# Moving the down-projection's weight combinations in four pieces, loading raw w_down one section ahead, and reordering the last groups of an attention-plus-GeGLU kernel

## The chip, the cores and the metric

The kernel runs on one core of a Trainium2 chip. The core has five engines that run side by side and meet at semaphores: TensorE (PE in the profile; its weight loads are PEld), VectorE (DVE), ScalarE (ACT), GpSimd (POOL) and SyncE (SP). In this kernel SP issues every DMA, one after the other, in the order of the program. The metric is the device time of one execution in microseconds (us), the median over several runs.

## The reference

With x of 2048 tokens by 576 features, all in float32:

```python
xn = layernorm(x)                                  # no scale, no bias
q, k, v = split(xn @ wqkv)                         # 32 heads of 18
s = softmax(q @ k.T * 18 ** -0.5) @ v  @ wo        # no mask
g = silu((gelu(xn @ w_gate) * (xn @ w_up)) @ w_down)   # hidden width 4608
out = x + s * g
```

## The kernel before

The float32 products are made of two reduced-precision parts each: a value is cut into a high part and a remainder, and three products (high with high, high with remainder, remainder with high) are summed in PSUM. Cutting is work of ACT, POOL and DVE.

**Prologue.** Layer norm, transposes, and the projections to q, k and v, whose results go to DRAM (`qk`, `vs`). The transposed, cut activations go to DRAM too (`xhs`).

**Sections.** The feed-forward part is cut into 144 sections: 4 token blocks of 512 tokens by 36 slices of 128 hidden columns. A section (`section`) multiplies one block with one slice of w_gate and w_up in 27 pairs of matmuls. Its number n gives the block b, the unit r (two slices, so 18 units for a block) and the half g of the unit: g = 0 is even n. Each section asks for the raw gate and up slices of section n + 2 (`load_gu`, 576 KB in two DMAs into two `raw` buffers) and has POOL (ACT in the lead) cut those of the next section, `split_gu`. Behind its pairs come the activation and `finish`, which sums and cuts the hidden values (`sums_a`, `cut_a`) into the tile A.

**Down products.** A unit's contribution to the output of the block is made by `down`: seven products instead of eight for a two by two split of the matrices, with combinations of quarters. They run one section after the unit's second one, so behind the even section of the next unit. The combinations of the w_down quarters are in the tile T: two precisions (index i) of seven combinations, 2016 KB. In block 0 the first five units (`PLAIN`) use the quarters as they are. The 18 units of `FORMED` (the other 13 units of block 0 and the first 5 of block 1) form T from the raw slice (`rawd`): `sums_b` on POOL makes the sums (`tsum`), `high_b` on ACT cuts the high parts, `low_b` on POOL the remainders, and `store_t` writes T to DRAM (`ts`). All other units read T back from there with `load_t`. Seven accumulators lie in M and are updated by DVE after each product; `combine` and `gates` bring them together at the end of a block and send them to DRAM (`ys`).

**Attention between the pairs.** From section 11 to section 138 the 27 pairs of a section have 8 score products (`score_pair`, their exponentials on ACT) and 8 products for the row maxima (`max_pair`, reduced by DVE) between them; the products with v (`values`) follow. All of them, the down products and the last projection take turns in three PSUM buffers (`ring`). Sections 0 to 10 are the lead, sections 139 to 143 the ends. Keys are loaded seven chunks ahead (`load_k`), and each such load waits for the scores of an older chunk, so SP walks through the program about one section at a time. The 32 units of attention results are normalised later: `load_scale` loads a unit and its reciprocal sums, `scale` multiplies on POOL, `store_scale` writes back (`on`).

**Block change.** In the last section of a block the activations of the next block are loaded (`load_xd`, six DMAs of 384 KB) and copied to the other half of the partitions by ACT and POOL (`copy_xd`).

**Ends.** Sixteen groups of 128 tokens are projected with wo (`project_o`, 28 matmuls each, after `split_o` has cut its input). `gate` takes tanh of the feed-forward result `yy`, `load_xy` loads x and `ys` of a group, and the sum goes to `out`. Twelve groups are spread behind the last sections, the block of the last four is special: its feed-forward result is still in M.

**What sets the order.** PE and SP run exactly in program order. The other engines' instructions are ordered ahead of time by a planner that simulates the program, apart from those marked `keep`, which stay in program order. A hook runs a piece of work in front of a given pair of the next section; on SP, where nothing waits for the pairs, a hook only sets a place in the queue.

## Time and profile before

| | |
|---|---|
| median of three runs | 2677.72 us (2675.94 to 2678.8) |
| profiled execution, its time | 2671.98 us |
| its span, first to last instruction | 2670.2 us |
| PE busy | 2573.9 us, 96% |
| DVE, POOL, ACT busy | 2146.0, 1585.5, 1476.0 us |
| mean granted PE clock | 0.988 |
| DMA | 442.85 MB, 166 GB/s |

Busy time of PE is the time in which at least one matmul is under way, so at 96% only about 96 us of the span are left in which it does nothing. A window row gives, for a stretch of time, its length, the busy time of each engine with the number of instructions, the granted clock, the mean busy share of the DMA engines and their rate. A timeline row gives start, duration, engine, line, operation and tiles, and in square brackets the idle time of the engine ahead of it and what ended it. A wait row gives who waited for whom, the total, how often, and the longest.

### The profile page before, as it was taken

The numbers are of one execution on the slowest core, as the hardware profiler recorded it, in microseconds if no ns is written. First come the engines' busy times: TensorE is split into PE (matmuls) and PEld (weight loads), VectorE is DVE, ScalarE is ACT, GpSimd is POOL, SyncE is SP. The second block draws the span as 40 slices with busy tenths as digits, with TensorE's granted clock in tenths as the row PEclk, the third lists the DMA queues.
The fourth block names the chain that finished last, engine by engine and source line by source line (L and its number), as shares of the span: only waits on it lengthen the run. The fifth ranks groups of instructions, "written<-read, shape, count | busy, mean of one in ns | idle before, by whom it ended". The sixth has DMA issues, their size and how long they took to land. (4 is left out here: it accounts for less than half of the span.)

```text
span 2670.2 us, 52622 instructions
## 1 busy us (share of the span) xinstructions
PE 2573.9 (96%) x20548; PEld 1850.8 (69%) x20548; DVE 2146.0 (80%) x2462; ACT 1476.0 (55%) x1783; POOL 1585.5 (59%) x1604
## 2 busy tenths in 40 slices
PE   9998999999999999999989999999999999999978
PEld 8886766666666666666656666666666666667667
DVE  5325788888887898999868989988987888997467
ACT  3223266666666655555556566666555656666522
POOL 2124478888788856566655655555566555555641
PEclk9999999999999999999989999999999999999989
DMA  8764355555566556665566555555565555554584
GB/s 263 260 222 128 92 150 161 156 161 156 156 178 177 164 174 166 166 165 165 165 150 176 166 157 156 156 156 156 156 171 159 160 148 158 157 158 139 143 248 143
DMA packets 378935, 442.85 MB, mean 166 GB/s; under 512 B 103484, under 2 KB 283196, under 8 KB 370112
## 3 DMA queue, kind: packets, MB, share of 16 engines
q1 hardware_dynamic: 378688, 439.49, 58.3%
q8 instruction: 163, 2.67, 0.4%
q14 instruction: 84, 0.69, 0.1%
HBM read 344.12 MB, written 95.26 MB: 165 GB/s over the span
## 5 line engine op out<-in xcount | busy, mean ns | idle before, releaser
L757 DVE TENSOR_REDUCE mx<-pm 128x2 f32<-128x1024 f32 x1024 | 1221.3, 1225 | 221.0 <-PE pm L756 201.8
L794 ACT ACTIVATE pT<-pe 128x1024 f32<-128x1024 f32 x1024 | 1047.4, 1027 | 611.0 <-PE pe L793 577.8
L421 PE MATMUL pu<-xd,wh 64*128 64x512 f32 x2538 | 931.7, 399 | 11.3 <-POOL xd L147 8.1
L421 PE MATMUL pg<-xd,wh 64*128 64x512 f32 x2538 | 931.3, 398 | 11.7 <-DMA xd<-xhs 6.0
L421 PEld LDWEIGHTS pg<-xd,wh 64*128 64x128 f32 x2538 | 471.2, 186 | 128.0 <-issue 60.3
L421 PEld LDWEIGHTS pu<-xd,wh 64*128 64x128 f32 x2538 | 470.9, 186 | 39.8 <-POOL xd L147 10.0
L421 PE MATMUL pg<-xd,wl 64*128 64x512 f32 x1269 | 498.4, 393 | 0.0
L421 PE MATMUL pu<-xd,wl 64*128 64x512 f32 x1269 | 497.8, 392 | 0.0
L106 POOL TENSOR_SCALAR wh<-raw 128x384 fp32r<-128x384 f32 x402 | 218.1, 547 | 448.2 <-DMA raw<-in_B_w_up_dram 234.3
L810 PE MATMUL acc<-pT,VS 128*32 128x512 f32 x4096 | 466.0, 595 | 0.0
L756 PE MATMUL pm<-KA,QT 64*128 64x512 f32 x2048 | 417.8, 396 | 16.3 <-ACT pT L794 15.4
L108 POOL TENSOR_TENSOR wl<-raw,wh 128x384 fp32r<-128x384 f32 x402 | 415.5, 1038 | 26.0
L793 PE MATMUL pe<-QT,KA 64*128 64x512 f32 x2048 | 418.3, 397 | 12.8 <-DVE mx L757 8.2
L533 PE MATMUL py<-T,ah 128*128 128x288 f32 x1876 | 384.7, 301 | 10.9 <-DVE M L537 8.5
L537 DVE TENSOR_TENSOR M<-py,M 128x576 f32<-128x576 f32 x448 | 338.9, 757 | 35.1 <-PE py L533 21.9
L533 PEld LDWEIGHTS py<-T,ah 128*128 128x128 f32 x1876 | 300.9, 190 | 66.6 <-issue 56.3
L450 POOL TENSOR_TENSOR al<-h,ah 128x512 fp32r<-128x512 f32 (+1 forms) x139 | 286.3, 2060 | 83.0 <-ACT ah L447 58.3
L810 PEld LDWEIGHTS acc<-pT,VS 128*32 128x32 f32 x4096 | 120.1, 109 | 276.7 <-issue 229.7
L793 PEld LDWEIGHTS pe<-QT,KA 64*128 64x128 f32 x2048 | 196.4, 185 | 130.1 <-DVE mx L757 29.3
L533 PE MATMUL py<-T,al 128*128 128x288 f32 x938 | 277.2, 296 | 2.4 <-POOL al L450 2.4
L421 PEld LDWEIGHTS pg<-xd,wl 64*128 64x128 f32 x1269 | 235.8, 186 | 32.3
L756 PEld LDWEIGHTS pm<-KA,QT 64*128 64x128 f32 x2048 | 202.5, 186 | 66.5 <-ACT pT L794 24.7
(155 smaller groups left out, 2984.0 us busy)
## 6 DMA issues: line engine op xcount, KB each, us to landing
T<-ts SPq DMA_DIRECT2D x49, 2016.0 KB
KA<-qk SPq DMA_DIRECT2D x768, 72.0 KB
raw<-in_B_w_gate_dram SPq DMA_DIRECT2D x144, 288.0 KB
raw<-in_B_w_up_dram SPq DMA_DIRECT2D x144, 288.0 KB
ts<-T SPq DMA_DIRECT2D x18, 2016.0 KB
VS<-vs SPq DMA_DIRECT2D x128, 152.0 KB
qk<-t SPq DMA_DIRECT2D x72, 256.0 KB
QT<-qk SPq DMA_DIRECT2D x192, 72.0 KB
```

What stands on the lines that cost most here:

```text
L106: first = nc.gpsimd.tensor_scalar(hi, raw, 1.0, 1.0, op0=ALU.mult, op1=ALU.mult)
L108: keep(nc.gpsimd.tensor_tensor(lo, raw, f(hi), op=ALU.subtract))
L421: nc.tensor.matmul(o, w[1 + wp][k][rr, c, :], xd[k][xp][rr, c, :], start=(i == 0), stop=(i == len(terms) - 1))
L450: keep(two.tensor_tensor(lo, raw, f(hi), op=ALU.subtract))
L533: nc.tensor.matmul(py[:, t, 0:DC], h[:, i, tt], T[:, w, k], start=n == 0, stop=n == 2)
L537: nc.vector.tensor_tensor(M[:, m], py[:, :, 0:DC], M[:, m], op=ALU.add)
L756: nc.tensor.matmul(pm[:, a], QS[u, r][rr, t * P:(t + 1) * P], KS[(u * NA + c) % KB][r][rr, :], start=True, stop=True)
L757: nc.vector.tensor_reduce(MX[u][:, 2 * r:2 * r + 2, t, c], pm, axis=AX.X, op=ALU.max)
L793: nc.tensor.matmul(pe[:, a], KS[(u * NA + c) % KB][r][rr, t * P:(t + 1) * P], QS[u, r][rr, :], start=True, stop=True)
L794: nc.scalar.activation(PT[u, kt][:, 2 * r:2 * r + 2, :], pe, AF.Exp, scale=SCALE)
L810: nc.tensor.matmul(ACC[u][32 * a:32 * a + 32, :], VS[(u * NA + c) % VB][:, v:v + 32], pt[:, a, :], start=first, stop=last, skip_group_chec ...
```

## The change

Eight things are changed, in the order of the program:

- `load_k(0)` and `load_q(0)`, 14 DMAs on SP, stand behind section 0 and its loads instead of ahead of them.
- Raw w_down of unit r + 1 is loaded in `finish` of the second section of unit r (`load_rawd`), not at the start of the next section behind its `load_gu`. `sums_b` is hooked to pair 12 instead of 22.
- T moves in four pieces (`PIECES`: for each precision the combinations 3 to 6 and then 0 to 2). The store is spread: the high parts at pairs 13 and 20 of the unit's second section, the remainders at pairs 2 and 9 of the section after it. The load has its first piece where the whole load stood and three at pairs 5, 13 and 21 of the next section. For the last unit of a block (blocks 1 and 2), all four pieces go one section later, to pairs 1, 6, 11 and 16 of the first section of the next block.
- The tiles of `load_scale` have two slots; it is called ahead of a section's maxima and down products, not near a block change; `scale` comes behind the down products of the next section instead of ahead of its maxima.
- The last reciprocal has a tile of its own (`t2`), and its store to DRAM is issued behind section 139 instead of ahead of the loads of the ends.
- Two groups of x and `ys` instead of one are loaded at the start of the ends; a group's load stands behind the projection of the group two earlier. `yy` has three buffers, and holds the gated product; `th` has one.
- The last unit's down products stand in front of all four groups of the last block instead of behind the first of them, then the four gates.
- The last block's groups are finished one at a time by DVE straight from PSUM, with one add and one store each.

```diff
+NEXT = [(0, r) for r in range(1, PLAIN)] + FORMED + [(0, NR)]
+PIECES = ((0, 3, 7), (0, 0, 3), (1, 3, 7), (1, 0, 3))
...
-    def load_t(r):
-        nc.sync.dma_start(f(FF["T"]).rearrange("p i m d -> p (i m d)"), ts[r])
+    def t_piece(r, k, store=False):
+        i, a, b = PIECES[k]
+        t, d = f(FF["T"])[:, i, a:b].rearrange("p m d -> p (m d)"), ts[r][:, (7 * i + a) * DC:(7 * i + b) * DC]
+        nc.sync.dma_start(*((d, t) if store else (t, d)))
...
+    def load_rawd(r):
+        FF["rawd"] = ffn.tile([P, G, D], F32, name="rawd")
+        nc.sync.dma_start(FF["rawd"], w_down[r * G * P:(r + 1) * G * P, :].rearrange("(g p) n -> p g n", p=P))
...
-        hooks, FF["hooks"] = FF["hooks"], {}
+        hooks, FF["hooks"], FF["next"] = FF["hooks"], FF["next"], {}
...
-        if g == 0 and (b == 0 or (b, r) in FORMED):
-            raw = FF["rawd"] = ffn.tile([P, G, D], F32, name="rawd")
-            nc.sync.dma_start(raw, w_down[r * G * P:(r + 1) * G * P, :].rearrange("(g p) n -> p g n", p=P))
-            if (b, r) in FORMED:
-                hook(22, lambda: sums_b(raw))
+        if n == 0:
+            load_rawd(0)
+        if g == 0 and (b, r) in FORMED:
+            raw = FF["rawd"]
+            hook(12, lambda: sums_b(raw))
...
+        if g == 1 and (b, r + 1) in NEXT:
+            load_rawd((r + 1) % NR)
...
+                for k, i in enumerate((13, 20)):
+                    hook(i, lambda k=k: t_piece(r, k, True))
...
-                store_t(r)
+                for k, i in enumerate((2, 9)):
+                    hook(i, lambda k=k: t_piece(r, 2 + k, True))
...
-                load_t(r)
+                late = (n + 2) % (NR * G) == 0 and n + 2 < NF
+                for k, i in enumerate((1, 6, 11, 16) if late else (None, 5, 13, 21)):
+                    if i is None:
+                        t_piece(r, k)
+                    else:
+                        hook(i, lambda k=k: t_piece(r, k), ("hooks", "next")[late])
...
+        if not SC:
+            SC.extend(ffn.tile([P, 2, TB], F32, name=m, tag=t) for m, t in (("on", "rawd"), ("od", "tsum")))
...
         def last_sums(u, rt):
-            rec = att.tile([P, QD, TB], F32, name="rec", tag="pT", bufs=4)[:, 0, :]
+            rec = ffn.tile([P, TB], F32, name="rec", tag="t2")
             tc.keep_in_program_order(nc.vector.reciprocal(rec, SUM[u]))
-            nc.sync.dma_start(rt, rec.rearrange("(a p) t -> a p t", p=32)[:, 0, :])
+            todo["rec"] = [lambda: nc.sync.dma_start(rt, rec.rearrange("(a p) t -> a p t", p=32)[:, 0, :])]
...
-        load_k(0)
-        load_q(0)
...
+            if n == 0:
+                load_k(0)
+                load_q(0)
...
+            if FF["n"] % G == 1 and (scaled + 1) * NA + 4 < n and SCALED <= n < NU * NA - 2 and 2 < FF["n"] % (NR * G) < NR * G - 2:
+                load_scale(scaled)
+                at(n + 1, 2, scale, scaled)
+                at(n + 2, 0, store_scale, scaled)
+                scaled += 1
...
-            if n >= SCALED and FF["n"] % G == 1 and (scaled + 1) * NA + 4 < n < NU * NA - 2:
-                load_scale(scaled)
-                at(n + 1, 0, scale, scaled)
...
-                nc.vector.scalar_tensor_tensor(th, th, 1.0, yy, op0=ALU.add, op1=ALU.mult)
+                nc.vector.scalar_tensor_tensor(yy, th, 1.0, yy, op0=ALU.add, op1=ALU.mult)
...
-                S2[j] = epi.tile([P, 2, DC], F32, name="s", tag=("yy", "th")[j % 2], bufs=2)
-                nc.scalar.activation(S2[j], po[:, :, 0:DC], AF.Copy, scale=0.25)
+                t = epi.tile([P, D], F32, name="last", tag="yy", bufs=3)
+                for c in range(2):
+                    m = QUARTERS[2 * (j // 2) + c][2]
+                    nc.vector.scalar_tensor_tensor(t[:, DC * c:DC * c + DC], FF["M"][:, m, j % 2], 0.25, po[:, c, 0:DC],
+                                                   op0=ALU.mult, op1=ALU.mult)
+            (nc.vector if (b, j) == groups[-1] else nc.gpsimd).tensor_tensor(xx, xx, t, op=ALU.add)
...
+        load_xy(*groups[0])
         load_wo()
+        load_xy(*groups[1])
...
+        def step():
+            nonlocal n
+            n += 1
+            ready()
+            project_o(*groups[n - 1])
+            if n + 1 < len(groups):
+                load_xy(*groups[n + 1])
+            if n > 1:
+                store()
...
+            if i == 0:
+                todo.pop("rec")[0]()
...
-        for k in range(TB // P):
-            if k == 1:
-                downs(then)
-            n += 1
-            ready()
-            project_o(*groups[n - 1])
+        downs({6: ((6, sub, 3),), 0: ((6, add, 0), (5, add, 0), (5, add, 2)), 4: ((6, sub, 4), (4, add, 2)),
+               1: ((5, sub, 1), (1, sub, 3))})
         M = FF["M"]
-        TG = [ffn.tile([P, 2, 2, DC], F32, name="tg", tag=tag) for tag in ("rawd", "tsum")]
-        for q, (i, c, m) in enumerate(QUARTERS):
-            t = TG[q // 2][:, q % 2]
+        for i, c, m in QUARTERS:
+            t = ffn.tile([P, 2, DC], F32, name="tg", tag=("h0", "h1")[c], bufs=2 - c)
             nc.scalar.activation(t, M[:, m], AF.Tanh, scale=0.25)
-            nc.vector.scalar_tensor_tensor(t, t, 1.0, M[:, m], op0=ALU.add, op1=ALU.mult)
-            for a in range(2):
-                j = 2 * i + a
-                nc.vector.tensor_tensor(t[:, a], t[:, a], S2[j][:, c], op=ALU.mult)
-                xx = XY[NB - 1, j][0][:, DC * c:DC * c + DC]
-                (nc.vector, nc.gpsimd)[a].tensor_tensor(xx, xx, t[:, a], op=ALU.add)
-                if c == 1:
-                    nc.sync.dma_start(out[S - TB + j * P:S - TB + (j + 1) * P, :], XY[NB - 1, j][0])
+            nc.vector.scalar_tensor_tensor(M[:, m], t, 1.0, M[:, m], op0=ALU.add, op1=ALU.mult)
+        for k in range(TB // P):
+            step()
+        store()
```

More of the change, by code (lines that the diff above doesn't have):

```diff
@@ L392 @@
     ps = ctx.enter_context(tc.tile_pool(name="ps", bufs=1, space=PSUM, reuse_waits="tile"))
-    FF = {"w": ahead, "xd": XD, "down": [], "gates": [], "n": 0, "hooks": {}, "raw": {},
+    FF = {"w": ahead, "xd": XD, "down": [], "gates": [], "n": 0, "hooks": {}, "next": {}, "raw": {},
           "M": ffn.tile([P, 7, 2, DC], F32, name="M"),
@@ L622, in finish, with hook @@
         FF.pop("last", lambda: None)()
-        def hook(i, what):
-            FF["hooks"].setdefault(i, []).append(what)
+        def hook(i, what, ahead="hooks"):
+            FF[ahead].setdefault(i, []).append(what)
+        if g == 1 and (b, r + 1) in NEXT:
+            load_rawd((r + 1) % NR)
         if b == 0 and r < PLAIN:
@@ L661, in tasks @@
             t()
-    SC = {}
+    SC = []
     def load_scale(u):
@@ L922, in load_xy @@
             rows = slice(b * TB + j * P, b * TB + (j + 1) * P)
-            XY[b, j] = [epi.tile([P, D], F32, name=m, bufs=n) for m, n in (("xx", 4), ("yy", 2), ("th", 2))[0:3 - 2 * (b == NB - 1)]]
+            XY[b, j] = [epi.tile([P, D], F32, name=m, bufs=n) for m, n in (("xx", 4), ("yy", 3))[0:2 - (b == NB - 1)]]
             for t, a in zip(XY[b, j], (x, ys)):
@@ L929, in gate @@
             if b < NB - 1:
-                xx, yy, th = XY[b, j]
+                yy = XY[b, j][1]
+                th = epi.tile([P, D], F32, name="th")
                 nc.scalar.activation(th, yy, AF.Tanh, scale=0.25)
-                nc.vector.scalar_tensor_tensor(th, th, 1.0, yy, op0=ALU.add, op1=ALU.mult)
+                nc.vector.scalar_tensor_tensor(yy, th, 1.0, yy, op0=ALU.add, op1=ALU.mult)
         def project_o(b, j):
-            rows = slice(b * TB + j * P, b * TB + (j + 1) * P)
             po = ring("po")
```

51 lines of the change are left out of this document (17 added, 34 removed).

## The prediction

> **What bounds the kernel now.** I read the head of the page first, then the waits of PE, then windows by stage, then the timelines of SP, POOL and ACT where PE stood still.
>
> ```profile
> PE 2573.9 (96%) x20548; PEld 1850.8 (69%) x20548; DVE 2146.0 (80%) x2462; ACT 1476.0 (55%) x1783; POOL 1585.5 (59%) x1604
> ```
> ```profile
> PE pm L756 <- ACT pT L794: 15.4, 14, 5.1
> PE py L533 <- DVE M L537: 8.5, 5, 6.6
> ...
> PE py L533 <- DMA T<-ts: 1.9, 1, 1.9
> ```
> ```profile
> 203.80:218.80 15.00, 8.61 (x56) 6.80 (x58) 1.98 (x3) 7.60 (x12) 9.78 (x8) 0.77 0.81 196
> 333.00:346.00 13.00, 7.91 (x50) 6.19 (x52) 6.32 (x7) 6.11 (x8) 12.37 (x11) 0.74 0.33 79
> 465.60:487.10 21.50, 19.70 (x164) 14.14 (x168) 17.36 (x20) 11.64 (x15) 16.75 (x17) 1.00 0.45 112
> 500.90:520.40 19.50, 19.50 (x164) 14.25 (x163) 17.44 (x20) 12.04 (x16) 16.56 (x17) 1.00 0.44 112
> 759.00:775.90 16.90, 15.54 (x122) 9.00 (x122) 11.68 (x12) 15.43 (x20) 15.45 (x17) 1.00 0.94 254
> 1371.50:1402.90 31.40, 18.65 (x122) 11.51 (x118) 11.56 (x12) 15.36 (x19) 17.22 (x19) 0.73 0.64 125
> 1992.90:2015.10 22.20, 17.83 (x122) 11.04 (x118) 11.60 (x12) 15.57 (x21) 16.44 (x18) 0.85 0.77 156
> 2054.80:2088.00 33.20, 33.20 (x282) 22.98 (x278) 23.53 (x24) 24.86 (x32) 19.07 (x23) 1.00 0.54 148
> 2512.40:2526.40 14.00, 11.03 (x74) 7.96 (x66) 7.27 (x10) 3.02 (x6) 13.42 (x14) 0.88 0.15 43
> 2526.40:2538.90 12.50, 12.50 (x109) 11.35 (x108) 7.97 (x10) 1.23 (x2) 4.03 (x5) 1.00 0.53 191
> 2538.90:2555.00 16.10, 7.67 (x45) 7.47 (x44) 9.74 (x14) 3.07 (x4) 0.00 (x0) 0.79 1.11 286
> 2577.30:2598.20 20.90, 14.05 (x88) 13.43 (x86) 14.36 (x19) 5.92 (x9) 10.38 (x10) 0.84 0.81 241
> 2612.10:2623.40 11.30, 11.30 (x88) 11.13 (x86) 8.12 (x11) 2.80 (x4) 3.96 (x2) 1.00 0.72 261
> 2629.80:2643.30 13.50, 11.52 (x84) 11.20 (x85) 9.01 (x13) 4.33 (x6) 1.47 (x1) 1.00 0.49 151
> 2643.30:2662.40 19.10, 17.58 (x128) 16.69 (x126) 18.93 (x30) 5.50 (x9) 3.62 (x3) 1.00 0.15 46
> ```
>
> PE is the bound: in the steady pair of sections (2054.8 to 2088.0) it is busy for all of the 33.2 us. No edit can gain there. What can be gained is where PE waits, and the halved clock that follows: the granted clock, third from the end, is well under 1.00 in every window with a long wait. So the change is priced place by place.
>
> **The change, part by part.** *Start.* PE ends section 0 at 203.8 and needs the raw slice of section 1.
>
> ```profile
> 198.34 2.12 SPq L724 DMA_DIRECT2D KA<-qk  x6
> ...
> 204.40 0.65 SPq L126 DMA_DIRECT2D raw<-in_B_w_up_dram  x1
> ```
> ```profile
> 209.33 1.35 ACT L112 ACTIVATE wh<-raw 128x384 fp32r<-128x384 f32 x3 [1.03 <-DMA raw<-in_B_w_up_dram]
> ```
> Fourteen DMAs that stand ahead of it go behind it, so the slice is issued some 5.4 us earlier, from 198.34 on, and lands at about 203.9. Its first cuts leave PE a wait of some 1.7 us, instead of 6.4 (15.0 less 8.61 busy). Without the halved clock the section takes 6.25 (half of the 12.50 for the two from 2526.4 on). Gain: 15.0 - 6.25 - 1.7 = 7.0. Section 1 covers the moved DMAs; if it did not, section 2 would wait for its keys. Bounds: 2 (a part of the wait) and 8.7 (all).
>
> *Forming stage, 18 units, up to about 950 us.*
>
> ```profile
> 469.93 0.51 POOL L106 TENSOR_SCALAR wh<-raw 128x384 fp32r<-128x384 f32 x1 [6.82 <-DMA raw<-in_B_w_up_dram]
> ...
> 473.09 1.43 POOL L482 TENSOR_TENSOR tsum<-rawd 128x576 f32<-128x576 f32 x1
> ...
> 475.86 0.81 POOL L484 TENSOR_TENSOR tsum<-rawd 128x288 f32<-128x288 f32 x1
> ```
> ```profile
> 475.94 1.17 ACT L490 ACTIVATE T<-tsum 128x1152 fp32r<-128x1152 f32 x1 [8.07 <-POOL tsum L483]
> ```
> POOL stands 6.8 us for a raw slice that is queued behind the 2 MB store of T, and only then makes the sums for which ACT waits 8.1; the exponentials queue behind that, and PE waits for them. Afterwards most of the store stands behind the raw slice, raw w_down is there a section earlier, and the sums come 10 pairs earlier. The stalled section (21.5) should become the quiet one (19.5). Of PE's 15.4 us of waits for exponentials, 5.1 belong to the next point; I leave 1.3 for what is not of this chain. Gain: 9.0. Bounds: 0 (nothing moves) and 10.3. The sums, 3.6 us from first to last row, now come ahead of other POOL work; the 4.7 us that POOL is idle in the window from 465.6 cover them. If that cover is gone, the cut hidden values are late (third rival).
>
> *First attention section* (333 to 346).
>
> ```profile
> 337.52 1.16 ACT L490 ACTIVATE T<-tsum 128x1152 fp32r<-128x1152 f32 x1 [7.77 <-POOL tsum L483]
> ```
> The same chain: PE waits 5.1 us, and a clock of 0.74 over 13 us means 6.8 us at half speed. Raw w_down now stands ahead of the raw slices in SP's queue, so the sums can start about 4 us earlier. I leave 1.1 us of the wait. Gain: 4.0, and 1.9 of clock (some 3.8 of the halved time lie behind the wait): 5.9. Bounds: 0 and 7.
>
> *Block changes at 1372 and 1993.*
>
> ```profile
> 1361.24 0.33 SPq L475 DMA_DIRECT2D T<-ts  x1
> ...
> 1367.16 8.64 SPq L140 DMA_DIRECT2D xd<-xhs  x6
> ```
> ```profile
> 1375.32 1.26 POOL L680 TENSOR_TENSOR on<-on,od 128x512 f32<-128x512 f32 x1 [8.96 <-DMA od<-rT]
> ```
> T, and at 1372 a scale load, stand ahead of the block's activations, and POOL, blocked for 9 us by that scale, copies them late. The change takes both away. The block change at 759, where no T is loaded, takes 16.9: that is my price for the others. New is that T is loaded in the next section and wanted at its end. SP's last activation load is out at 1375.8, near the start of that section; some eight more DMAs stand ahead of T, so T starts about 6 us in, needs with a raw slice (2.65 MB at 286 GB/s) 9 to 10, and lands at 16 to 18, when the down products come, about 17 us in: 1 us of wait each. Gains: 31.4 - 16.9 - 1.0 = 13.5 and 22.2 - 16.9 - 1.0 = 4.3. Bounds: 6 to 14.5, and 0 to 5.3.
>
> *Steady stage.* Three more DMA issues for each of 49 loads, some 0.3 to 0.6 us each, and the two scale slots cost nothing: SP spends far more waiting for scores.
>
> ```profile
> SPq L724 <- PE pe L793: 655.3, 118, 13.3
> ```
> The first piece waits for four of seven products only, so SP is free sooner; what stands behind it, raw slices above all, gains. T has most of a section to spare there.
>
> A page speaks against the change: the Trainium skill, "DMA: Bandwidth & Descriptors", section "Bandwidth", says to batch DMAs to at least 1 MiB, and its section on the anatomy of one DMA gives each a fixed 2 us. By that, as an estimate, three more DMAs in a load that is waited for would cost 6 us at three places, and the sum would be 18 us smaller. This trace does not show it so far: from 2538.9 to 2555.0 transfers of 144 to 2016 KB together ran at 286 GB/s.
>
> *Before the ends* (2512.4 to 2526.4). POOL, held by a scale, cuts the hidden values late: 3.0 us of waits (14.0 less 11.03), and 1.7 of clock (half of the 3.4 us that 0.88 stands for). The scale goes behind the down products, and the raw slice ahead of three pieces of T. Gain: 4.7. Bounds: 0 and 4.7.
>
> *Ends.*
>
> ```profile
> 2530.56 0.56 SPq L837 DMA_DIRECT2D rT<-rec  x1
> 2531.21 0.39 SPq L475 DMA_DIRECT2D T<-ts  x1
> ```
> ```profile
> 2542.91 0.76 DVE L932 SCALAR_TENSOR_TENSOR th<-th,yy 128x576 f32<-128x576 f32 x1 [6.52 <-ACT th L931]
> ```
> ```profile
> T<-ts SPq DMA_DIRECT2D x49, 2016.0 KB
> ...
> woh<-wos SPq DMA_DIRECT2D x1, 1152.0 KB
> ```
> SP stood until 2530.56 for the last reciprocal. Without that, the loads start 7 us earlier, counted from section 139. But three pieces of T now stand behind both parts of wo (2.8 MB with their rests), two groups of x and `ys`, and a raw slice: 6.6 MB with T, 23 us at 286 GB/s. T is complete about 21 us after the start of section 139; PE wants it after 12.5. So the waits of 1.9 for T and 6.6 for DVE (which was held by the late `ys`) become one of about 8. Gain: 0. Bounds: -5 and 8.
>
> Groups 4 to 6 take 20.9 us, where three later ones take 11.3: DVE waits for `ys`, with the next group's `ol` behind it. SP reaches group 2's load some 10 us earlier relative to PE, since two scale slots end its wait for a store. I leave 2 us. Gain: 7.6. Bounds: 0 and 9.6.
>
> From the end of section 143 (2629.8) to that of the span it took 40.4 us.
>
> ```profile
> 2661.63 5.96 SPq L1009 DMA_DIRECT2D out_dram<-xx  x4
> ```
> Now: two groups 7.5, a wait of 1.5 for the cut hidden values (three groups covered it before), down products and four groups 23.0 (19.1 for the former and three groups, and one more at 3.8); then a multiplication of half a group, an add, a DMA issue, about 1.6 together, and the landing, 2.6 (from 2667.6). Together 36.2. Gain: 4.2. DVE's share there, 18.93 of 19.1, makes it a bound beside PE, so the bounds are -4 and 6.
>
> **Sum.** 7.0 + 9.0 + 5.9 + 13.5 + 4.3 + 4.7 + 0 + 7.6 + 4.2 = 56.2. The profiled execution took 2671.98 us (span 2670.2); it would take 2615.8. The median of the runs shown, 2677.72, is 5.7 above it; on that scale 2621.
>
> **Rivals.** *The pieces come late where they are waited for.* Whole, T took 9.6 us from its issue (2531.2) to the end of PE's wait for it. Counting that in place of 7 behind a raw slice, the two late loads are some 3 us later, with 1.7 of clock: 8 for both. At the ends it is another 4 late, and groups 4 to 6 keep their chain, 7.6. Together 20 less: 2641. For it speaks the order of the queue, against it SP's earlier start. The page's rule above would lead here too.
>
> *The planner does not follow.* In the rows above, POOL cuts two raw parts (from 469.93) ahead of the sums, though in the program the sums come first. If it does so again, and ACT waits as before, the forming stage, the first attention section and the 4.7 give nothing: 19.6 less, 2641.
>
> *Slower: POOL becomes the bound of the forming stage.* If the sums go ahead of the cut of the hidden values, that cut is 3.6 us later in each of 18 units.
>
> ```profile
> 458.57 2.96 POOL L450 TENSOR_TENSOR al<-h,ah 128x1280 fp32r<-128x1280 f32 x1
> ```
> ```profile
> 469.08 0.53 PE L533 MATMUL py<-T,ah 128*128 128x288 f32 x2
> ```
> It ended at 461.5, and the products that use it begin at 469.1: 7.6 us are spare, 4 after the sums. From about 7 us of delay on it decides: PE would wait 3 us in each unit, 54 in all, more than the other terms give (56.2 - 9.0 = 47.2). With 4 us each, 72 - 47 = 25 over before: 2703. Against it stands the idle time of POOL.
>
> **How the numbers follow.** Likeliest case 0.63, its own range 2604 to 2636; late pieces 0.20; planner 0.08; POOL 0.09. The range of 2600 to 2652 takes in the first three and leaves out the last and the tails. About 0.2%, 5 us, is what a measurement of this kernel can tell from no change. Faster 0.88 (the first three, 0.91, less 0.03 for both of the middle ones at once with a worse end), same 0.03, slower 0.09.
>
> **What would show it.** Right: no wait of ACT for `tsum` over 5 us; the windows of the last sections of a block near 17 us; one wait of PE for T, about 8 us, after section 140. Wrong: PE waiting for `al` in the forming stage, for T over 3 us in the first section of a block, for `ol` between groups 4 and 6 as before, or anywhere in the steady pair, which must stay at 33.2.

## The result, and the profile after

The changed kernel took 2642.24 us (median; 2636.63 to 2644.3), the kernel before 2677.93 us on the same chip. The ratio is 0.9864, with a 95% interval of 0.9847 to 0.9882: 1.4% faster. The profiled execution took 2643.16 us, its span 2641.4 us. By the medians 35.7 us of the 56.2 that the prediction added up came, by the two traces 28.8. (The traced execution before, 2671.98 us, lies below the range of the others, and the traced one after above its median; so the sums below, made from the traces, come out some 7 us under the medians.) The question of the experiments is where the rest went.

PE has the same work as before (2572.5 us busy, 20548 matmuls), and 97% of the span instead of 96%.

The change was priced place by place, so it is read place by place. Windows of the changed kernel (start and end, length, busy time of PE, PEld, DVE, ACT and POOL with counts, granted clock, DMA share, GB/s), cut at the same points of the program as the windows in the prediction:

```profile
205.20:211.80 6.60, 6.39 (x58) 4.95 (x54) 1.98 (x3) 5.73 (x9) 5.11 (x6) 1.00 0.48 140
211.80:219.40 7.60, 6.69 (x56) 5.18 (x58) 3.01 (x4) 3.68 (x8) 7.60 (x7) 1.00 0.60 167
317.70:337.60 19.90, 18.25 (x143) 14.65 (x143) 18.17 (x21) 11.73 (x15) 14.05 (x14) 1.00 0.75 187
337.60:739.00 401.40, 400.64 (x3340) 275.68 (x3336) 364.92 (x396) 265.57 (x307) 329.59 (x314) 1.00 0.57 165
739.00:756.10 17.10, 15.47 (x117) 9.08 (x117) 12.05 (x12) 15.60 (x20) 15.89 (x18) 1.00 0.98 230
756.10:787.50 31.40, 23.99 (x165) 16.15 (x169) 23.65 (x24) 11.96 (x15) 23.27 (x21) 0.89 0.34 111
1358.60:1376.90 18.30, 16.67 (x122) 10.57 (x118) 11.99 (x12) 15.59 (x20) 14.80 (x17) 0.91 0.92 239
1376.90:1402.30 25.40, 21.89 (x164) 15.43 (x160) 22.46 (x24) 9.84 (x13) 13.93 (x12) 0.93 0.53 151
1974.10:1991.00 16.90, 15.64 (x122) 8.88 (x123) 11.86 (x12) 15.60 (x20) 14.52 (x17) 1.00 0.89 222
2352.90:2368.70 15.80, 14.07 (x122) 8.56 (x121) 15.34 (x18) 9.87 (x13) 13.22 (x13) 1.00 0.43 113
2492.40:2501.40 9.00, 9.00 (x76) 6.39 (x68) 7.71 (x10) 3.13 (x6) 5.26 (x7) 1.00 0.21 58
2513.90:2531.10 17.20, 7.86 (x45) 7.64 (x44) 8.62 (x11) 2.10 (x4) 7.10 (x10) 0.70 0.90 202
2552.30:2564.90 12.60, 11.60 (x88) 11.21 (x86) 9.79 (x12) 5.13 (x7) 5.70 (x5) 1.00 0.86 281
2571.20:2583.90 12.70, 8.03 (x45) 7.83 (x44) 7.84 (x12) 1.80 (x3) 1.79 (x2) 0.73 0.34 111
2601.50:2641.40 39.90, 31.39 (x210) 30.49 (x210) 29.88 (x45) 8.01 (x11) 8.46 (x5) 0.90 0.28 98
```

Windows of the kernel before that the prediction did not need:

```profile
218.80:225.15 6.35, 6.35 (x60) 5.61 (x58) 2.15 (x4) 3.59 (x7) 2.02 (x2) 1.00 0.75 204
325.00:350.40 25.40, 19.69 (x143) 16.08 (x143) 18.38 (x21) 11.59 (x14) 16.28 (x16) 0.87 0.48 105
350.40:759.00 408.60, 402.32 (x3342) 275.96 (x3344) 362.09 (x396) 263.84 (x308) 324.48 (x312) 1.00 0.57 163
775.90:799.30 23.40, 20.29 (x164) 14.19 (x166) 21.87 (x24) 11.79 (x15) 20.27 (x17) 1.00 0.39 102
1402.90:1426.50 23.60, 20.34 (x164) 14.13 (x168) 22.04 (x24) 9.85 (x12) 14.37 (x13) 1.00 0.63 187
2374.90:2388.60 13.70, 13.70 (x122) 8.76 (x119) 12.81 (x18) 9.83 (x12) 10.27 (x10) 1.00 0.53 115
2604.50:2612.20 7.70, 6.23 (x45) 5.81 (x44) 6.73 (x10) 1.80 (x3) 0.00 (x0) 1.00 0.41 147
```

Set side by side, in us (before, after, gain; the prediction's gain last). In the first row the second number is section 2. The second number of the forming stage is what lies behind the section after its block change (799.3 to 951.6 before, 787.5 to 937.8 after).

| place | before | after | gain | predicted |
|---|---|---|---|---|
| start, sections 1 and 2 | 15.0 + 6.35 | 6.6 + 7.6 | 7.15 | 7.0 |
| first attention section | 25.4 | 19.9 | 5.5 | 5.9 |
| forming stage without its block change | 408.6 + 152.3 | 401.4 + 150.3 | 9.2 | 9.0 |
| section behind the first block change | 23.4 | 31.4 | -8.0 | 0 |
| block change at 1372, and the section behind it | 31.4 + 23.6 | 18.3 + 25.4 | 11.3 | 13.5 |
| block change at 1993 | 22.2 | 16.9 | 5.3 | 4.3 |
| steady sections that end an attention unit | | | -10.4 | 0 |
| before the ends | 14.0 | 9.0 | 5.0 | 4.7 |
| ends, products of the first unit | 16.1 | 17.2 | -1.1 | 0 |
| groups 4 to 6 | 20.9 | 12.6 | 8.3 | 7.6 |
| ends, products of the second unit | 7.7 | 12.7 | -5.0 | 0 |
| from section 143 to the end | 40.4 | 39.9 | 0.5 | 4.2 |

The steady row is a difference: from the end of the forming stage (951.6 before, 937.8 after) to the last attention section (2512.4 and 2492.4) the kernel gained 6.2, and the block changes in it 16.6. The pair from 2030.6 to 2063.8 is untouched at 33.2; the loss sits in sections like the one from 2352.9, 15.8 instead of 13.7. These are the sections in which one of the 32 units of attention results ends, every fourth one; in eleven of them the changed kernel is 0.5 to 2.1 us slower. The remaining 1 us are small places (the prologue, -1.4; sections 3 to 9, +1.5; the first block change, -0.2; groups 0 to 3, +1.1).

So the forecast gains came where they were forecast, but for the last, and three places lost what nobody had priced.

In the forming stage the waits went much as forecast. PE's for exponentials fell from 15.4 us to 3.6. ACT's for the sums of w_down, in the kernel before and then in the changed one:

```profile
ACT T L490 <- POOL tsum L483: 75.5, 12, 8.1
```
```profile
ACT T L494 <- POOL tsum L487: 3.9, 1, 3.9
```

For its cuts, POOL stood 61.6 us for raw slices between 350 and 950 us of the kernel before; in the changed kernel that wait is gone.

**First block change.** POOL's timeline of the changed kernel there:

```profile
755.41 1.40 POOL L486 TENSOR_TENSOR tsum<-rawd 128x576 f32<-128x576 f32 x1
...
758.97 0.60 POOL L149 CAST xd<-xd 64x512 fp32r<-64x512 f32 x1
```

The last copy of the new block's activations hangs at pair 15 of the section; the sums moved from pair 22 to pair 12, so 3.5 us of them now stand in front of it. PE waited 3.7 us for `xd`, and the clock was halved behind it (0.89 over the window).

**Steady sections that end an attention unit.** There DVE works on the unit's row maxima (`nm`, `m`) in a chain of small operations. DVE and then POOL of the changed kernel, in the section from 2352.9:

```profile
2356.63 0.98 DVE L776 CAST m<-nm 128x16 fp32r<-128x16 f32 x1
2357.65 1.19 DVE L777 TENSOR_TENSOR m<-nm,m 128x16 fp32r<-128x16 f32 x1
```
```profile
2354.20 0.99 POOL L108 TENSOR_SCALAR wh<-raw 128x384 fp32r<-128x384 f32 x2 [5.12 <-DMA raw<-in_B_w_up_dram]
...
2357.54 1.27 POOL L461 TENSOR_TENSOR h<-h,h 128x512 f32<-128x512 f32 x1
```

The same instructions in the kernel before, DVE and POOL:

```profile
2377.96 0.17 DVE L766 TENSOR_TENSOR m<-nm,m 128x16 fp32r<-128x16 f32 x1
```
```profile
2378.16 1.30 POOL L680 TENSOR_TENSOR on<-on,od 128x512 f32<-128x512 f32 x1 [8.37 <-DMA od<-rT]
```

Before, POOL stood 8.4 us for `od` while DVE ran its chain of small operations, and these took 0.17 us each. After, POOL cuts the raw slice and adds hidden values beside that chain, and the same operations take 0.98 and 1.19; L777 ends when POOL's L461 ends. `accs` is evicted late, and PE waits for its ring buffer: 7.4 us in 11 places instead of 1.7 in 2.

The kernel before has the other case too. In eleven of 21 unit ends (from 1003 us on) POOL multiplies a scale first and the subtraction (L766) takes 0.17; each of these sections lasts 13.7 us. In eight others the scale comes late and POOL's first sum of hidden values runs beside the subtraction; each of these lasts 14.2. (The two left lasted 14.2 and 15.2, with POOL at work beside the subtraction as well.) One of the eight, as window, DVE and POOL:

```profile
1493.40:1507.60 14.20, 14.07 (x122) 8.57 (x126) 13.72 (x18) 9.83 (x12) 10.97 (x10) 1.00 0.48 109
```
```profile
1496.50 1.27 DVE L766 TENSOR_TENSOR m<-nm,m 128x16 fp32r<-128x16 f32 x1
```
```profile
1496.46 1.28 POOL L459 TENSOR_TENSOR h<-h,h 128x512 f32<-128x512 f32 x1 [8.14 <-DVE m L765]
```

**The second unit of the ends.** ACT and DVE of the changed kernel:

```profile
2574.78 0.68 ACT L944 ACTIVATE th<-yy 128x576 f32<-128x576 f32 x1 [5.73 <-DMA yy<-ys]
```
```profile
2575.55 0.76 DVE L945 SCALAR_TENSOR_TENSOR yy<-th,yy 128x576 f32<-128x576 f32 x1 [3.35 <-ACT th L944]
```

The wait for `ys` that had held group 6 now holds group 7: its gate stands on DVE ahead of the additions to M (the first at 2576.83), so PE waits 4.7 us for those, with 6.8 us of halved clock (0.73 over 12.7).

**The end.** DVE of the changed kernel runs without a gap:

```profile
2611.82 3.45 DVE L538 TENSOR_TENSOR M<-py,M 128x576 f32<-128x576 f32 x5
...
2623.97 0.28 DVE L930 TENSOR_TENSOR oh<-KA,oh 64x128 fp32r<-64x128 f32 x1
```

PE waits 2.9 us for that `oh`, and the clock is halved for 6.8 us behind it.

### The profile page after: what moved, and what is told of

Its sections match the earlier page's. It is cut to its first block, busy times and chain, and to the rows that moved or that the text cites. A ratio compares the mean times of both kernels' runs of the same rounds, so it can differ in the third digit from the quotient of the medians.

```text
span 2641.4 us, 52882 instructions
## 1 busy us (share of the span) xinstructions
PE 2572.5 (97%) x20548; PEld 1847.5 (70%) x20548; DVE 2164.7 (82%) x2459; ACT 1476.0 (56%) x1779; POOL 1580.3 (60%) x1603
## 4 chain that ended last, share of the span: by engine, by line
PE 86%; DVE 7%; DMA 3%; ACT 1%; POOL 1%; issue 1%; SPq 1%; DVEq 0%; POOLq 0%; ACTq 0%
PE pg L423 20%; PE py L534 14%; PE acc L821 13%; PE pu L423 11%; PE pe L804 9%; PE pm L767 8%; PE po L183 7%; DVE mx L768 1%; DMA T<-ts 1%; PE po L954 1%; DVE m L777 1%; PE py L521 1%; DVE h L440 1%; DVE h L433 1%; DVE accs L827 1%
## 5 line engine op out<-in xcount | busy, mean ns | idle before, releaser
L110 POOL TENSOR_TENSOR wl<-raw,wh 128x384 fp32r<-128x384 f32 x402 | 410.2, 1023 | 27.7
L538 DVE TENSOR_TENSOR M<-py,M 128x576 f32<-128x576 f32 x448 | 339.0, 758 | 34.5 <-PE py L534 19.9
L423 PEld LDWEIGHTS pu<-xd,wl 64*128 64x128 f32 x1269 | 235.3, 185 | 14.4
```

The source lines that it names most:

```text
L110: keep(nc.gpsimd.tensor_tensor(lo, raw, f(hi), op=ALU.subtract))
L423: nc.tensor.matmul(o, w[1 + wp][k][rr, c, :], xd[k][xp][rr, c, :], start=(i == 0), stop=(i == len(terms) - 1))
L538: nc.vector.tensor_tensor(M[:, m], py[:, :, 0:DC], M[:, m], op=ALU.add)
```

## Experiments

All start from the changed kernel. Ratios are to the kernel before, run on the same chip; the changed kernel's own is 0.9864 (0.9847 to 0.9882). A step of 0.001 is 2.7 us, and the intervals reach some 4 to 5 us to either side; what is smaller is read from windows. Many of these kernels leave most stages as they are, so the same stage is seen in several executions.

**The scale put back.**

```diff
             tasks(n, 0)
-            if FF["n"] % G == 1 and (scaled + 1) * NA + 4 < n and SCALED <= n < NU * NA - 2 and 2 < FF["n"] % (NR * G) < NR * G - 2:
-                load_scale(scaled)
-                at(n + 1, 2, scale, scaled)
...
             finish()
+            if FF["n"] % G == 1 and (scaled + 1) * NA + 4 < n and SCALED <= n < NU * NA - 2 and 2 < FF["n"] % (NR * G) < NR * G - 2:
+                load_scale(scaled)
+                at(n + 1, 0, scale, scaled)
```

> The scale's load goes back behind the down products and its multiplication back to the head of the next section (the guard near block changes and the two slots stay). Theory: in the steady stage the changed kernel loses some 10 us in eleven sections that end a unit, because POOL no longer stands for `od` at the end of the section and so cuts the raw slice beside DVE's chain of small operations; DVE's 0.17 us copy takes 0.98 there and `accs` comes late (six waits of PE for `accs`, 6.2 us). With POOL held again the waits fall to one or two, 1.5 us in all, and the time from 2642 to about 2634. Rival: the raw slice is late because three pieces of T share the bandwidth with it; then the waits stay and the time is within 2 us of 2642.

0.9875 (0.9859 to 0.9892): no gain, and PE waited 8.8 us for `accs`, in 11 places as in the changed kernel. The theory fell, in this form. POOL does wait for `od` again, 76.6 us in 31 places (151.3 in 18 in the kernel before, 8.4 in 7 in the changed one), but too early to be cover:

```profile
2349.77 1.29 POOL L693 TENSOR_TENSOR on<-on,od 128x512 f32<-128x512 f32 x1 [2.19 <-DMA od<-rT]
```

`od` is used 8.8 us after its issue instead of 12.6, with one piece of T ahead of it in the queue instead of the whole. The multiplication is over before the section ends (its last pair at 2352.6; in the kernel before it began 3.3 us behind that pair), and POOL still cuts the raw slice in front of the sums of the hidden values. The scale back together with T whole was not run.

**T whole in the steady units.**

```diff
+                if not late and n in ATT:
+                    nc.sync.dma_start(f(FF["T"]).rearrange("p i m d -> p (i m d)"), ts[r])
-                for k, i in enumerate((1, 6, 11, 16) if late else (None, 5, 13, 21)):
+                for k, i in enumerate((1, 6, 11, 16) if late else () if n in ATT else (None, 5, 13, 21)):
```

> In the steady stage T is loaded whole again, where its first piece is now; the two units before a block change and the ends keep the pieces. Theory of POOL: the raw slice still comes near the end of the section, POOL still cuts it beside DVE's chain, and the six waits for `accs` stay or grow: 2642 to 2650. Rival, the pieces share the bandwidth with the raw slice: the waits go, and the time falls by about 8 to 2634.

0.9868 (0.9853 to 0.9882). PE's waits for `accs` went from 7.4 us to 1.2, and the unit-end section from 15.8 to 14.2. The rival's number; but not its reason, as POOL's timeline of this kernel shows:

```profile
2348.07 1.28 POOL L461 TENSOR_TENSOR h<-h,h 128x512 f32<-128x512 f32 x1 [6.84 <-DVE m L778]
...
2355.12 0.99 POOL L108 TENSOR_SCALAR wh<-raw 128x384 fp32r<-128x384 f32 x2
```

The raw slice is not cut earlier. It is cut later: with T in one piece the planner sets the cuts behind the hidden values' sums and cuts, as it did in the kernel before, and with T in four it sets them in front (2354.20 against 2357.54 above). So the loss is an order on POOL that the smaller pieces led the planner to. The 14.2 that remains against 13.7 is the sums beside DVE's subtraction (1.27 us here too): POOL's wait for `od` and the multiplication had kept them later. In this kernel's trace that costs 4.8 of the 10.4 over all unit ends. No run brought that part back; that this is its cause rests on the two cases inside the kernel before, 13.7 and 14.2. By the ratios the time hardly moved, but their intervals leave room for the 5.6 us of the unit ends, and the ends lost part: with T first there, PE stood 9.4 us for the additions to M instead of 9.3 for T.

**The sums behind the copy.**

```diff
-            hook(12, lambda: sums_b(raw))
+            hook(20 if (b, r) == (1, 0) else 12, lambda: sums_b(raw))
```

> In the first unit of the second block alone, the sums of w_down go from pair 12 to pair 20, behind POOL's last copy of the block's activations (pair 15). Theory: the 3.73 us wait of PE for `xd` at 755.9 and the 3.4 us of halved clock after it go, so 5.4 us less, 2637; the waits of 1.4 and 2.1 for DVE later in that section stay. Rival: the sums are then late in their turn, ACT and the exponentials stall as they did in the kernel before, and the section keeps its 31.4 us: 2642.

0.9838 (0.9824 to 0.9853), some 7 us less. The wait for `xd` at 756 is gone; the section takes 25.8 instead of 31.4:

```profile
757.20:783.00 25.80, 21.94 (x164) 15.50 (x168) 22.92 (x24) 12.08 (x16) 23.67 (x20) 0.93 0.42 130
```

One edit that the prediction had booked as free cost a fifth of what the whole change gained.

**T whole before the two block changes.**

```diff
+                if late:
+                    nc.sync.dma_start(f(FF["T"]).rearrange("p i m d -> p (i m d)"), ts[r])
-                for k, i in enumerate((1, 6, 11, 16) if late else (None, 5, 13, 21)):
+                for k, i in enumerate(() if late else (None, 5, 13, 21)):
```

> In the two units before the block changes at 1369 and 1985 T is loaded whole again at the end of the section before, as in the kernel before; the scale load stays away from the block changes. Theory (the prediction's): T ahead of the block's activations costs 5 us at 1985, and at 1369 most of the 13: in all 12 us more, 2654, with PE waiting for `xd` in both places. Rival: at 1369 it was the scale load alone, which is away here too: then about 5 more, 2647.

0.9922 (0.9902 to 0.9942): some 15 us lost by the ratios, 11 by the medians. The two windows:

```profile
1358.20:1384.40 26.20, 17.33 (x122) 10.62 (x120) 11.84 (x12) 15.50 (x21) 16.46 (x18) 0.80 0.64 129
1980.20:2002.30 22.10, 16.36 (x122) 10.05 (x120) 12.26 (x12) 15.56 (x20) 16.68 (x18) 0.92 0.75 152
```

At 1980 all of the 5.3 is given back (22.1; it was 22.2), at 1358 7.9 of 13.1. T ahead of the block's activations was a cost at both, at the second the whole of it. The other 5.2 at the first are what is left for the scale load, which was not put back there alone. That step of the prediction holds.

**The ends: `ys` ahead of x.**

```diff
-            for t, a in zip(XY[b, j], (x, ys)):
+            for t, a in list(zip(XY[b, j], (x, ys)))[::-1]:
```

> Each group's load takes `ys` ahead of x. Theory: in the ends the load of x stands in SP until the store of the group four before has landed, `ys` is behind it (issued at 2569.4, used at 2574.8), DVE stands for it with the additions to M behind, and PE waits 4.67 us at 2573, with 6.8 us of halved clock. With `ys` ahead that wait goes: 7 to 8 us less, 2634 (on the scale of 2642). Rival: DVE is itself full there, so the wait stays within 1 us and the time too.

0.9858 (0.9838 to 0.9877), the rival's time: PE's wait for the additions was 6.0 us there. But DVE was not full: it stood 3.8 us for that gate. SP had stood 3.1 us for POOL's addition of an earlier group, which held the buffer of the `ys` before; the `ys` of group 7, in SP's queue at 2558.9, then took until 2566.1 to be used, 7.2 us, where it had taken 5.8 in the changed kernel.

**The ends: T first, group 0's gate behind the products.**

```diff
-                    if i is None:
+                    if i is None or n == ATT.stop - 1:
...
-            split_o(b, j)
-            gate(b, j)
+            if n or not OP:
+                split_o(b, j)
+            if not early:
+                gate(b, j)
...
             if i == 1:
-                ready()
+                ready(early=True)
             downs()
+            if i == 1:
+                ready()
```

> At the last unit before the ends all four pieces of T are issued ahead of x, `ys` and wo, and the gate of group 0 (the product with `ys`) goes behind the down products in the program; its cut values stay in front. Theory: the 9.35 us wait for T at 2514 is one of SP's order alone, 10.2 us of halved clock with it; both go, wo is there in time, and the time falls by 12 to 14, to 2629. Rival: what must arrive, 6.6 MB, sets the time; the wait then moves to the output projection, for wo or for the gate, and no more than 4 us are gained: 2638.

0.9856 (0.9841 to 0.987), not to be told from the changed kernel, and the wait for T became one of 7.3 for the additions to M. ACT of this kernel shows what they stood for:

```profile
2514.53 0.68 ACT L944 ACTIVATE th<-yy 128x576 f32<-128x576 f32 x1 [4.20 <-DMA yy<-ys]
```

It is the gate of group 1 now, in front of the section's activation and of everything that needs it.

**The last combinations on POOL.**

```diff
-                nc.vector.tensor_tensor(M[:, to], M[:, to], M[:, by], op=op)
+                (nc.gpsimd if to == 5 else nc.vector).tensor_tensor(M[:, to], M[:, to], M[:, by], op=op)
```

> Of the eight combinations behind the last down products, the three into M's sixth part go from DVE to POOL. Theory: DVE is the bound from 2611 to 2624 (it runs without a gap), so 2.0 us less on DVE take 2 us off PE's 2.94 us wait for `oh` and, with the halved clock behind it, up to 5 off the time: 2638. Rival: POOL does them slower and beside DVE, and the gate that needs them holds DVE: the same, 2642, or 2 us more.

0.9875 (0.9858 to 0.9892): no gain, the rival. POOL took 1.83 to 1.87 us for each, where DVE takes 0.75; two of DVE's own combinations beside it took 1.32, and PE still waited 2.8.

**Five edits together:** T whole in the steady units and at the first unit of the ends, the sums behind the copy, `ys` first, group 0's gate behind, three combinations on POOL.

> Together: T whole in the steady units and at the last unit before the ends, the sums of the second block's first unit behind the last copy, `ys` ahead of x, the gate of group 0 behind the down products, the three combinations on POOL. If the terms are independent: 5.6 (steady waits, as measured with T whole), 5.7 (the copy), 7 (`ys`), 12 (T at the ends), 2 (DVE at the end): 32 less than 2642, 2610. If the waits of the ends only move, 2625.

0.9818 (0.9802 to 0.9834), 2626 us: faster than both kernels, 12 us below the changed one, with an interval that does not touch its own. The sum of the parts had said 32. The steady stage and the block change gave theirs (the section behind it took 24.2); the ends kept a wait of 7.7 for the additions.

**The ends: every gate behind the additions, T first.**

```diff
+                after(nc.scalar.activation(th, yy, AF.Tanh, scale=0.25), FF["M_add"], "additions first")
+                after(nc.vector.scalar_tensor_tensor(yy, th, 1.0, yy, op0=ALU.add, op1=ALU.mult), FF["M_add"],
+                      "additions first")
...
             for k in range(GROUPS[i]):
-                step()
+                step(k == GROUPS[i] - 1)
```

The last group of each stretch cuts the next one's operand, and that one's gate comes behind the next down products.

> As with T first (all four pieces at the last unit before the ends ahead of x, `ys` and wo), and every gate of a group, ACT's tanh and DVE's product, is ordered behind the additions to M before it, so that no gate that waits for `ys` stands ahead of them. Theory: both long waits of the ends are DVE's and ACT's order, a late `ys` being what they stand for; at 2510 PE's wait of 7 to 9 and 6.8 to 10.2 us of halved clock go, at 2565 its wait of 5 to 6 and 3.4 to 6.8 of clock: 14 less in all, 2627. Rival: what must arrive is too much in any order; the waits move to the output projection: 2638.

0.9854 (0.9837 to 0.9871). Both long waits of the ends shrank to 1.3 and 0.5, and a new one of 11.2 us came between them. Windows of this kernel (the products of the first unit, groups 0 to 3), then a wait of SP:

```profile
2511.50:2519.40 7.90, 6.29 (x45) 5.86 (x44) 7.52 (x10) 1.35 (x3) 0.00 (x0) 1.00 1.12 278
2519.30:2547.50 28.20, 16.99 (x114) 16.48 (x112) 12.88 (x17) 5.37 (x8) 16.04 (x15) 0.78 0.77 199
```
```profile
SPq L700 <- POOL on L693: 9.6, 1, 9.6
```

The products take 7.9 instead of 17.2. With T first and only group 0's gate behind them a wait of 7.3 had stayed, so what held the products then was the order of ACT and DVE. But SP stands 9.6 us, up to 2529.5, for POOL's scale before it stores it, the load of group 2 is behind, and DVE stands 13.2 us for its gate.

**The scales behind the first groups,** with this order of the ends, T whole in the steady units and the sums back at pair 22:

```diff
             if i == 0:
                 todo.pop("rec")[0]()
-            if 0 < i <= NU - scaled:
-                scale(scaled + i - 1)
-                store_scale(scaled + i - 1)
-            if i < NU - scaled:
-                load_scale(scaled + i)
+                for u in range(scaled, NU):
+                    load_scale(u)
...
+            if i == 1:
+                for u in range(scaled, NU):
+                    scale(u)
+                    store_scale(u)
```

> The order of the ends as in the run with the gates behind the additions, and the last two scales loaded together (there are two slots), multiplied and stored behind the first four groups; with it T whole in the steady units and the sums back at pair 22. Theory: in the ends every one of the waits was one for `ys` (or T) behind something in SP's queue; with the gates behind the additions the wait of 11.2 us for `oh` at 2532 came from SP standing from 2519 to 2529.5 for POOL's scale, with the group's `ys` behind. With the scales behind the groups that wait and 13.7 us of halved clock go: 18 less there than in that run. With 7 from the sums and 3 from T whole: 2610. Rival: the ends are full, by DVE or by what must arrive; the wait appears again at the next group, and only the 10 are gained: 2625.

0.9822 (0.9808 to 0.9835), 2627 us: as good as the five edits and no better; the rival. SP no longer stands ahead of it, and still `ys` of group 2, issued at 2517.95, was not used before 2527.8. ACT and a window of this kernel:

```profile
2527.80 0.68 ACT L946 ACTIVATE th<-yy 128x576 f32<-128x576 f32 x1 [12.44 <-DMA yy<-ys]
```
```profile
2490.00:2528.00 38.00, 30.41 (x239) 27.14 (x237) 24.20 (x31) 6.46 (x10) 13.46 (x16) 0.98 0.89 258
```

From the first load of the ends to that moment the DMA engines are 0.89 busy and move 258 GB/s. With the orders of ACT, DVE and SP out of the way, the transfers are what the rows still show: T, wo, raw slices, two scales and three groups in 38 us. PE's two waits for `ol` and `oh` there were still 8.5 us. One limit of the program is left in all these orders: a DMA waits in SP for the one issued eight places before it (in the changed kernel a raw slice stands 3.6 us for `woh`, with three pieces of T behind it). More DMAs under way were not tried, and that no order could do better is not shown.

Over the whole of the ends no order gained anything that can be told from the spread of single traces. From the last pair of section 138 to that of section 143 the changed kernel took 109.4 us (117.7 before), the kernels of this section that leave the ends as they are 107.3 to 112.8, and those with another order 106.1 to 112.3.

**What made the forming stage's gain.** Two of its three edits were undone, one at a time:

```diff
-            hook(12, lambda: sums_b(raw))
+            hook(22, lambda: sums_b(raw))
```

> In all formed units the sums of w_down go back from pair 12 to pair 22; raw w_down stays a section ahead and the store in four pieces. Theory: the earlier sums are what ends the stalls of ACT; the forming sections give back at least 4 of the 8.5 us gained, and the first attention section some, while the block change at 756 gains 5.4: 2640 to 2644. Rival: the early load and the spread store did it; then the forming sections stay within 1 us in sum, and with the block change mended the time is 5 lower, 2635.

```diff
-                for k, i in enumerate((2, 9)):
-                    hook(i, lambda k=k: t_piece(r, 2 + k, True))
+                nc.sync.dma_start(ts[r], f(FF["T"]).rearrange("p i m d -> p (i m d)"))
```

> In the formed units T is stored whole again at the end of the second section; the sums stay at pair 12, raw w_down a section ahead. Theory: the 2 MB store stands ahead of the raw slice, POOL stands for that slice again and cuts it late; the forming stage gives back 4 to 8 us: 2648. Rival: with raw w_down there early the sums need no raw slice first, and the store costs nothing: 2642.

0.9841 (0.9822 to 0.986) and 0.9862 (0.9842 to 0.9882). The stage from its second attention section to the block change, first with the sums at pair 22, then with the whole store:

```profile
337.20:738.80 401.60, 400.79 (x3340) 277.57 (x3336) 364.66 (x396) 265.67 (x308) 329.81 (x314) 1.00 0.56 164
755.70:779.90 24.20, 20.36 (x164) 14.16 (x164) 22.85 (x24) 11.99 (x15) 23.34 (x20) 1.00 0.47 144
```
```profile
338.20:739.30 401.10, 400.34 (x3340) 274.08 (x3340) 359.64 (x396) 265.80 (x307) 324.09 (x314) 1.00 0.57 167
```

401.6 and 401.1, where the changed kernel has 401.4 and the kernel before 408.6: neither edit is needed. What is left is raw w_down a section ahead. That it does it alone was not run; either of the others could stand in for the other one. The first attention section, too, kept its gain in both (19.8 us by its last pairs, 19.6 in the changed kernel). With the other two edits in place the earlier sums gained nothing, and they are what cost the 8.0 at the block change (24.2 with the sums back).

## Why the prediction was right, and where it was wrong

The time came out inside the range, but that is in part luck. The range reached down to 2652 for two rivals at 2641, late pieces and a planner that does not follow, and neither came true: T was on time at the block changes, and the forming stage gained its 9.2 us. What brought the time from 2621 to 2642 are costs that the sum had at nothing, or sized wrongly, told below.

- **Start, first attention section, forming stage: right in size** (21.9 of 21.9; at the start the wait that was left came in section 2, not in section 1). The mechanism of the forming stage was right in part: ACT's waits for the sums went from 75.5 us to 3.9 and POOL no longer stands for the raw slice, but the spread store and the earlier sums, which the prediction counted too, could each be undone at no cost. PE never waits for `al`, the sign of the third rival.
- **Block changes at 1372 and 1993: right**, 13.1 and 5.3 for 13.5 and 4.3, and T was there in the next section: PE has no wait for it. (The 1.8 lost in the section behind the first is clock, 0.93.) The quiet block change at 759 was the right price for the others (17.1, 18.3, 16.9; the one that took 18.3 here took 16.9 or 17.0 in the eleven other kernels that keep the pieces there).
- **Before the ends, groups 4 to 6: right**, 5.0 and 8.3.
- **"One wait of PE for T, about 8 us, after section 140": right.** It was 9.3, with 10.2 us of halved clock, and the gain there 0 (-1.1 in the products, then +1.1 in groups 0 to 3).
- **The sums "come ahead of other POOL work; the 4.7 us that POOL is idle cover them": wrong at the block change.** There the quoted window had POOL 15.43 busy in 16.9. The prediction took that window, at 759, as the price of an undisturbed block change, while the change moved the sums ahead of the last copy right behind it. Term: 0; measured -8.0, of which the undo gives 5.6 to 7.2.
- **"Steady stage: nothing": wrong.** PE cannot gain there, but it can lose. POOL's 8 us for `od` were counted as harm at one block change and not seen as cover at the unit ends, and that the planner moves POOL's cuts when T gets smaller was not asked. The pair that was to stay at 33.2 did; it is not one in which an attention unit ends. Measured -10.4 in this trace; eight other traces with the same steady code lost 7.3 to 10.9 (without the section behind the second block change, where the clock differs).
- **Groups 4 to 6, "I leave 2 us": right for these groups, but not asked where the stall goes.** `ys` is late next for group 7, whose gate stands ahead of the additions: -5.0 at 2571.
- **From section 143: 4.2, measured 0.5.** The wait between the groups and the products was 0.8 for the expected 1.5, but DVE, given as a lower bound of -4, is the bound: 2.9 us of wait, and 3.4 lost to the halved clock behind it. In the run with `ys` ahead the same wait had no halved clock behind it, which is 2.6 us of the difference.
- **Smaller DMAs: no run shows the price of 18 us.** At the two block changes the four pieces were on time (the gains of 13.1 and 5.3 above), and at the ends PE waited 9.3 us for T where 8 was forecast without that price; in the steady units the pieces did harm through POOL's order, not through a late T. The 18 us were an estimate from the Trainium skill ("DMA: Bandwidth & Descriptors", sections "Bandwidth" and the anatomy of one DMA), which gives its 2 us for DMAs that GpSimd issues; here SP issues them.

## What to carry to other kernels

An engine's idle wait can be what keeps it out of another engine's way: before taking a wait away, look at what that engine will do in that time, and beside which short operations. When a step is moved earlier on an in-order engine, list what else hangs between its old place and its new one in every stage it runs in, the rare ones (a block change, the end) first. And when a late input is the cause of a stall, moving the stall's victim out of its way can just move the wait to the next consumer: here 9.3, then 7.3, then 11.2, then 7.2 us in four kernels.

## What was not expected of the hardware

- A DVE operation on 16 columns takes 0.17 us alone and up to 1.27 beside POOL, in the kernel before already (L766 at 2377.96 and at 1496.50): it lasts until the POOL operation that was running ends, within 0.03 us (L777 of the changed kernel, 2357.65 + 1.19, and POOL's 2357.54 + 1.27). The Trainium skill, "SBUF — State Buffer", section "SBUF: two separate sides", describes the port pair that both share as an exclusive lock held for a whole instruction; the trace agrees, for a subtraction with two inputs in SBUF.
- The same wait is followed by a halved clock in one execution and not in another. The wait for `oh` near the end, 2.9 to 3.0 us in both (the changed kernel, then the one with `ys` ahead, each from the start of the last down products on):

```profile
2608.90:2636.80 27.90, 23.99 (x156) 23.09 (x154) 22.43 (x34) 4.77 (x7) 6.73 (x5) 0.88 0.20 70
```
```profile
2600.00:2625.30 25.30, 21.35 (x156) 20.44 (x154) 22.44 (x34) 4.77 (x7) 6.75 (x5) 1.00 0.21 75
```

  Same counts, 2.6 us apart, and the clock alone is worth 3.4. In the 13 traces of the changed kernel and the experiments this wait is 2.8 to 3.0 us every time; behind it the clock is halved for 6.8 us in five, for 3.4 in three, and not at all in five. So a place that holds a wait of about 3 us can't be priced closer than some 3 us from one trace.
